# One score product, 16-tile value products, two-bank projections and a new PSUM bank plan in a recurrent attention kernel

## The chip, the cores and the metric

The kernel runs on one core of one Trainium2 chip. The metric is the device time of one execution in microseconds (us).

Engine names: PE is TensorE's matmul row, PEld its weight-load row, DVE is VectorE, ACT is ScalarE, SP is the queue that issues most of the DMAs. PSUM is the memory into which every matmul of these kernels writes (`ps` in the profile), used in banks by the program; SBUF is where the program keeps its other tiles. "L518" is line 518 of the kernel at hand; the lines of the two kernels differ, and the text says which stage a line is.

## The reference

A transformer block: layernorm, a recurrent attention with a small memory, a residual, layernorm, a gated feed-forward, a residual. Only the recurrence matters here:

```python
# S=2048 tokens, D=640, H=32 heads of Dh=128, M=8 memory tokens, segments of 32 tokens; all bf16
mem = mem0                                            # [1, 8, 640]
for s in range(64):
    h = concatenate([mem, x[:, 32*s : 32*s+32]])      # 40 tokens
    q, k, v = h@Wq, h@Wk, h@Wv                        # 32 heads x 128
    scores = q @ k.T * Dh**-0.5                       # 40 x 40 per head; mask: see below
    p = softmax(where(mask, scores, -1e9))            # memory rows see all, token rows memory + causal
    o = (p @ v) @ Wo                                  # 40 x 640
    mem = o[:, :8]                                    # goes into the next segment
    outs.append(o[:, 8:])
# ... then the feed-forward: h2 = h + (relu(n@W_gate) * (n@W_up)) @ W_down,  F = 1728
```

The loop is serial: segment s+1 needs `mem`, which is what the output projection of segment s made.

## The kernel before

One pass of the loop handles one segment. A pass projects the 8 memory tokens of its own segment together with 24 "rider" tokens of later segments, 32 in all; rings hold the riders' keys, queries and values (`Kr`, `Qr`, `Vr`). The tokens that don't fit (32 of every 128) are projected by "fillers", placed where TensorE would wait. In a pass, all but the transposes is cut into 32-column tiles of TensorE's array (`128*32`, `32*32` and `8*32` in the profile before; the transposes have `128*128`). A `Px` or `Pm` is an exponent of scores, `oT` the transposed attention output, `act_r` the transposed input of a pass.

Projection of one half (2048 of 4096 columns) into one PSUM bank, 20 matmuls of 512 columns, each with its own weight load:

```python
def qkv_bank(act, akeys, j, i, dst, dkey, eng):
    b = BQ[nq[0] % 2]                                  # two banks in turn
    nq[0] += 1
    def f(pe):
        for c in range(DC):                            # DC = 5
            for g in range(4):
                o = 2048 * i + 512 * g
                ins = pe.matmul(bank(b)[32 * g:32 * g + 32, :], act[:, c, :], W[:, j, c, o:o + 512],
                                start=(c == 0), stop=(c == DC - 1), skip_group_check=True)   # L330
    # ... then a copy of the bank to SBUF, on ACT and DVE in turn
```

Scores: two sweeps over the same keys, one with the 8 memory queries (`QmT`), one with the 32 rider queries (`Qr`); 64 load-matmul pairs each:

```python
def scores_mem(s):      # for k in 8, g in 4:
    pe.matmul(bank(BM)[..., k * 8:k * 8 + 8],      KmT[:, 4 * k + g, :],      QmT[:, 4 * k + g, :], ...)      # L469
    pe.matmul(bank(BM)[..., 64 + k * 8: ... + 8],  Kr[:, 4 * k + g, p:p + 32], QmT[:, 4 * k + g, :], ...)     # L472
    # Pm = exp(bank), then Pbd = min(Pm, block-diagonal mask)
def scores_x(s):        # for k in 8, g in 4:
    pe.matmul(bank(XS)[..., k * 32:k * 32 + 32],   Kr[:, 4 * k + g, p:p + 32], Qr[:, 4 * k + g, p:p + 32], ...)   # L536
    pe.matmul(bank(XS)[..., 256 + k * 32: ...],    KmT[:, 4 * k + g, :],       Qr[:, 4 * k + g, p:p + 32], ...)   # L539
    # Px = exp(bank), then causal min
```

Rider value products, 64 pairs on the four diagonal 32x32 tiles of the array, into three banks, then a reciprocal and a multiply per bank (L568, L579, L581):

```python
for k in ks:
    for a in range(2):                                 # a: memory keys or segment keys
        for g in range(4):
            pe.matmul(bank(XPB[k])[32 * g:32 * g + 32, o:o + 129], lh, rh, start=(a == 0), stop=(a == 1),
                      skip_group_check=True, tile_position=(32 * g, 32 * g))
```

The chain that closes the recurrence: output projection (L518, 128 pairs), copy of its bank to SBUF (L380), DVE transpose (L455), copy into `act_r` (L457). And the order of one pass:

```python
K, K, Q, Q, V            # projections, then trans8 of K and Q, then the second V half
scores_mem; filler 0 / half of woe; pv_mem; scores_x; filler 1 / half of woe
trans_om; trans_ox(s-1); wo_pass; to_act(s+1); pv_x(s); closing transpose of the filler
```

`woe` is the output projection of the leftover tokens, once in four passes (s mod 4 = 1); the layernorm of the next 128 rows is in the same pass.

The softmax here doesn't subtract the row's maximum and nothing guards it: scores larger than these inputs give would overflow.

## Time and profile before

The median is 1435.8 us (four executions, 1433.1 to 1438.6). The view by windows splits the profiled execution at the first projection of the first full pass and at the end of the last one. Columns: window, its length, then busy us (and instructions) of PE, PEld, DVE, ACT, POOL, then the granted clock, the DMA share and GB/s.

```profile
0.00:66.70 66.70, 33.72 (x756) 20.20 (x756) 17.07 (x51) 11.91 (x20) 4.11 (x21) 0.95 0.87 325
66.70:1187.50 1120.80, 1001.00 (x33927) 664.79 (x33923) 521.62 (x1449) 345.56 (x606) 0.00 (x0) 0.99 0.09 20
1187.50:1438.60 251.10, 219.79 (x1836) 118.21 (x1832) 92.28 (x189) 53.80 (x110) 0.00 (x0) 0.94 0.17 55
```

So 78% of the time is the passes: 1120.8 us, in which PE is busy 1001 us and DVE and ACT half of that or less. The chain that ended last, by engine, says the same:

```profile
PE 78%; DVE 7%; issue 6%; DMA 4%; ACT 3%; SPq 1%; POOL 0%; DVEq 0%; POOLq 0%
```

| before | us | from |
|---|---|---|
| start / passes / feed-forward | 66.7 / 1120.8 / 251.1 | windows |
| one pass, K projection to next K projection, mean of 62 | 18.08 | timeline |
| the same for s mod 4 = 1, 2, 3, 0 | 19.52, 18.23, 17.49, 16.96 | timeline |
| one projection matmul of 512 columns, start to start | 0.054 | timeline |
| one score sweep of 64 pairs | 0.53 | timeline |
| rider value product, 64 pairs, when undisturbed | 1.05 | timeline |

The groups of instructions, by shape, show the two score sweeps. The columns are line, engine, operation, tiles, shapes and count; then busy us and mean ns of one; then the idle time before them and what ended it.

```profile
L539 PE MATMUL ps<-Qr,KmT 128*32 128x32 bf16 x2048 | 45.3, 180 | 4.7 <-issue 4.6
...
L536 PE MATMUL ps<-Qr,Kr 128*32 128x32 bf16 x2048 | 44.6, 181 | 12.7 <-issue 12.7
...
L472 PE MATMUL ps<-QmT,Kr 128*32 128x8 bf16 x2016 | 40.7, 171 | 0.0
L469 PE MATMUL ps<-QmT,KmT 128*32 128x8 bf16 x2016 | 40.6, 171 | 2.0 <-issue 1.4
```

An 8-column matmul is listed with 171 ns and a 32-column one with 181 ns, yet 64 pairs take 0.53 us, 8.3 ns a pair. So the listed length is some 20 times what a pair adds, and four times the columns cost 10 ns of it.

Waits of PE, with total us, times and the longest:

```profile
PE ps L568 <- issue: 27.7, 30, 1.6
...
PE ps L518 <- DVE oT_102 L380: 22.6, 27, 2.7
...
PE ps L518 <- issue: 19.9, 20, 2.0
...
PE ps L536 <- issue: 12.7, 11, 1.6
...
PE ps L518 <- DVE oT_101 L380: 10.2, 31, 0.7
```

"Issue" means that nothing in the profile was waited for. These waits are odd: they fall into the middle of a matmul sequence. This is one, in a rider value product (timeline; start, duration, engine and group, and in brackets the idle time before it):

```profile
665.01 0.22 PE L568 MATMUL ps<-Vr_93,Px 32*32 32x129 bf16 x2
665.07 0.33 DVE L380 CAST wtok_108<-ps 128x160 bf16<-128x160 f32 x1 [2.19 <-PE ps L518]
665.43 0.35 DVE L455 STREAM_TRANSPOSE TBf<-wtok_108 128x160 bf16<-128x160 bf16 x1
665.81 0.17 DVE L457 COPY act_r_80<-TBf 128x40 bf16<-128x40 bf16 x1
666.12 0.09 PEld L568 LDWEIGHTS ps<-Vr_93,Px 32*32 32x32 bf16 x2 [1.07 <-issue]
```

The product stops after two matmuls for 1.07 us with everything it reads long there. Of the 80 "issue" gaps over 0.3 us in which both rows of TensorE stand, 79 are at the same place of its instruction order, number 193 modulo 256, counting loads, matmuls and the 107 semaphore instructions of its queue (without these the number drifts). And the page's list of DMA queues has an instruction queue that moved 285 packets of 16 KB (kind, packets, MB, share of the DMA engines):

```profile
q8 instruction: 285, 4.67, 1.3%
```

### The profile page before, as it was taken

How to read it: one execution, taken by the hardware profiler on the slowest of the kernel's cores; microseconds unless marked ns; L12 is line 12 of the kernel's file. 1: busy time of each engine (PE TensorE's matmuls, PEld its weight loads, DVE VectorE, ACT ScalarE, POOL GpSimd, SP SyncE). 2: the span in 40 equal slices, each digit the busy share in tenths (PEclk: the TensorE clock that was granted, in tenths of full speed). 3: DMA queues.
4: the chain of work that ended last, by engine and by line, in shares of the span. 5: the costliest groups of instructions: out<-in, count | busy, mean ns of one | idle time of the engine just before them, and what ended most of it. 6: DMA issues, size and time to landing. Idle time of an engine off the chain costs nothing.

```text
span 1438.6 us, 77225 instructions
## 1 busy us (share of the span) xinstructions
PE 1254.5 (87%) x36507; PEld 803.2 (56%) x36507; DVE 631.0 (44%) x1687; ACT 411.3 (29%) x736; POOL 4.1 (0%) x21
## 2 busy tenths in 40 slices
PE   1989898989898989898989898989898984899998
PEld 0555555655666556555656555556565653455454
DVE  2344444444444444444544454444454534334422
ACT  0223232323232323333333333333333321213311
POOL 1000000000000000000000000000000000000000
PEclk9999999999999999999999999999999997899999
DMA  9600000000000000000000000000000015110100
GB/s 368 236 16 22 18 21 18 21 18 22 18 22 18 22 18 22 17 21 18 22 18 22 19 21 18 21 18 22 18 20 18 17 39 202 40 37 24 51 19 19
DMA packets 44733, 58.21 MB, mean 40 GB/s; under 512 B 19264, under 2 KB 33280, under 8 KB 44416
## 3 DMA queue, kind: packets, MB, share of 16 engines
q1 hardware_dynamic: 40384, 42.80, 10.4%
q10 hardware_dynamic: 4032, 10.49, 2.0%
q8 instruction: 285, 4.67, 1.3%
q14 instruction: 32, 0.26, 0.1%
HBM read 35.48 MB, written 5.24 MB: 28 GB/s over the span
## 4 chain that ended last, share of the span: by engine, by line
PE 78%; DVE 7%; issue 6%; DMA 4%; ACT 3%; SPq 1%; POOL 0%; DVEq 0%; POOLq 0%
PE ps L330 23%; PE ps L518 13%; PE ps L350 11%; PE ps L804 8%; PE ps L364 6%; PE ps L568 5%; PE ps L826 5%; DMA W<-in_A_Wv_dram 3%; DVE tok_87 L337 1%; PE ps L539 1%; PE ps L493 1%; PE ps L536 1%; SPq L298 1%; PE ps L472 1%; ACT Kr L378 1%
## 5 line engine op out<-in xcount | busy, mean ns | idle before, releaser
L330 PE MATMUL ps<-W,act_r_81 128*32 128x512 bf16 x2680 | 156.1, 386 | 11.5 <-DMA W<-in_A_Wk_dram 8.5
L330 PE MATMUL ps<-W,act_r_80 128*32 128x512 bf16 x2560 | 149.6, 386 | 1.7 <-issue 1.6
L335 ACT ACTIVATE tok_84<-ps 128x512 bf16<-128x512 f32 x65 | 38.8, 597 | 362.1 <-PE ps L330 362.1
L330 PEld LDWEIGHTS ps<-W,act_r_81 128*32 128x32 bf16 x2680 | 69.8, 98 | 84.4 <-DMA W<-in_A_Wk_dram 8.8
L518 PE MATMUL ps<-Wo,oT_102 128*32 128x160 bf16 x4224 | 85.2, 238 | 27.8 <-DVE oT_102 L380 22.6
L330 PEld LDWEIGHTS ps<-W,act_r_80 128*32 128x32 bf16 x2560 | 67.7, 98 | 71.5 <-issue 8.9
L337 DVE CAST tok_87<-ps 128x512 bf16<-128x512 f32 x92 | 63.7, 692 | 98.4 <-PE ps L330 95.6
L581 DVE TENSOR_TENSOR ox<-ps,rx 128x384 bf16<-128x384 f32 (+1 forms) x192 | 98.5, 513 | 6.6
L518 PEld LDWEIGHTS ps<-Wo,oT_102 128*32 128x32 bf16 x4224 | 76.3, 99 | 35.8 <-DVE oT_102 L380 27.6
L518 PE MATMUL ps<-Wo,oT_101 128*32 128x160 bf16 x4224 | 83.9, 236 | 13.4 <-DVE oT_101 L380 10.2
L335 ACT ACTIVATE tok_86<-ps 128x512 bf16<-128x512 f32 x92 | 54.9, 597 | 116.6 <-PE ps L330 116.6
L350 PE MATMUL ps<-W,act_r_81 128*32 128x512 bf16 x1360 | 85.9, 380 | 1.9 <-issue 1.5
L518 PEld LDWEIGHTS ps<-Wo,oT_101 128*32 128x32 bf16 x4224 | 74.6, 98 | 22.0 <-DVE oT_101 L380 15.7
L350 PE MATMUL ps<-W,act_r_80 128*32 128x512 bf16 x1280 | 80.9, 380 | 0.0
L337 DVE CAST tok_85<-ps 128x512 bf16<-128x512 f32 x65 | 45.0, 692 | 69.7 <-PE ps L330 69.7
L378 ACT ACTIVATE Kr<-ps 128x768 bf16<-128x768 bf16 (+3 forms) x74 | 52.4, 724 | 38.5 <-DVE KmT L380 37.0
L544 ACT ACTIVATE Px<-ps 128x512 bf16<-128x512 f32 x64 | 38.2, 597 | 70.0 <-PE ps L539 70.0
L536 PE MATMUL ps<-Qr,Kr 128*32 128x32 bf16 x2048 | 44.6, 181 | 12.7 <-issue 12.7
L350 PEld LDWEIGHTS ps<-W,act_r_81 128*32 128x32 bf16 x1360 | 34.4, 96 | 34.8 <-issue 2.0
L518 PE MATMUL ps<-Wo,oTe 128*32 128x160 bf16 x2048 | 43.2, 233 | 11.8 <-issue 11.8
L378 ACT ACTIVATE Qr<-ps 128x768 bf16<-128x768 bf16 (+3 forms) x74 | 52.1, 723 | 1.5 <-PE ps L364 1.5
L539 PE MATMUL ps<-Qr,KmT 128*32 128x32 bf16 x2048 | 45.3, 180 | 4.7 <-issue 4.6
(193 smaller groups left out, 2077.3 us busy)
## 6 DMA issues: line engine op xcount, KB each, us to landing
attn_d<-wtoke SPq DMA_DIRECT2D x256, 2.5 KB
W<-in_A_Wk_dram ACTq DMA_DIRECT2D x1, 2560.0 KB
W<-in_A_Wq_dram ACTq DMA_DIRECT2D x1, 2560.0 KB
W<-in_A_Wv_dram ACTq DMA_DIRECT2D x1, 2560.0 KB
Wo<-in_A_Wo_dram ACTq DMA_DIRECT2D x1, 2560.0 KB
W<-in_A_Wk_dram SPq DMA_DIRECT2D x1, 2560.0 KB
W<-in_A_Wq_dram SPq DMA_DIRECT2D x1, 2560.0 KB
W<-in_A_Wv_dram SPq DMA_DIRECT2D x1, 2560.0 KB
```

Of the source, the lines that this page charges most:

```text
L330: ins = pe.matmul(bank(b)[32 * g:32 * g + 32, :], act[:, c, :], W[:, j, c, o:o + 512], start=(c == 0), stop=(c == DC - 1), skip_group_chec ...
L335: add("act", lambda a: a.activation(dst, bank(b), ACTF.Copy), r=[B(b)], w=[dkey])
L337: add("dve", lambda v: v.tensor_copy(dst, bank(b)), r=[B(b)], w=[dkey])
L350: ins = pe.matmul(bank(b)[32 * g:32 * g + 32, :], act[:, c, :], W[:, 2, c, o:o + 512], start=(c == 0), stop=(c == DC - 1), skip_group_chec ...
L364: ins = pe.matmul(bank_bf(b)[:, k * 128:(k + 1) * 128], t[:, (k % 4) * 128:(k % 4 + 1) * 128], ident[:, :], is_transpose=True)
L378: add("act", lambda a: a.activation(dst, src, ACTF.Copy), r=r, w=w)
L518: i = pe.matmul(bank(bk)[32 * gg:32 * gg + 32, 0:160], src[:, hb, :], w[:, gg], start=(hb == 0), stop=(hb == 31), skip_group_check=True)
L539: i = pe.matmul(bank(XS)[32 * g:32 * g + 32, 256 + k * 32:256 + k * 32 + 32], KmT[:, 4 * k + g, :], Qr[:, 4 * k + g, p:p + 32], start=True ...
L568: i = pe.matmul(bank(XPB[k])[32 * g:32 * g + 32, o:o + 129], lh, rh, start=(a == 0), stop=(a == 1), skip_group_check=True, tile_position=( ...
L581: add("dve", lambda v, src=src, k0=k0, n=n: v.tensor_tensor(ox[:, k0:k0 + n, :], src[:, :, 0:128], ap(rx, k0, [[1, n], [0, 128]]), ALU.mul ...
L804: ins = pe.matmul(bank(bk)[0:nf, :], w[:, c, j * 128:j * 128 + nf], xn2T[par][:, c, :], start=(c == 0), stop=(c == DC - 1))
L826: i = pe.matmul(bank(bk)[:, 0:320], hT[par][0:nf, j, u * 128:(u + 1) * 128], Wd[0:nf, j, hf * 320:(hf + 1) * 320], start=(j == 0), stop=(j ...
```

## The change

The intent is fewer and denser TensorE instructions and shorter waits:

1. One score product. The ring of queries keeps the 8 memory queries beside the 32 riders (`Qr` is [H, 3, 40]), so each key tile is loaded once and meets 40 columns: 64 pairs instead of 128.
2. Rider value products on all 16 tiles of 32x32, each row group into its own bank, with one reciprocal and two multiplies instead of three and three.
3. A projection does both halves, in two banks, with the same `act` tile; the second half's matmuls carry `ldweights=False` and use the tile that is loaded (`HOLD`). 40 loads fewer per pass.
4. The closing chain transposes straight from PSUM in fp32; the copy to SBUF rows goes to ACT, off the chain.
5. Filler evictions all on ACT; exponent of the memory scores ahead of the ring copy of the queries; the transposes of the layernormed rows behind `trans_ox`; `woe` as a filler unit. A new plan of the banks (`P0` to `P3`) makes room for all this.

```diff
+    def project(act, akeys, j, halves, banks):
         def f(pe):
             for c in range(DC):
-                for g in range(4):
-                    o = 2048 * i + 512 * g
-                    ins = pe.matmul(bank(b)[32 * g:32 * g + 32, :], act[:, c, :], W[:, j, c, o:o + 512], ...)
+                for n, i in enumerate(halves):
+                    for g in range(4):
+                        o = 2048 * i + 512 * g
+                        a = (bank(banks[n])[32 * g:32 * g + 32, :], act[:, c, :], W[:, j, c, o:o + 512])
+                        if n == 0 or not HOLD:
+                            ins = pe.matmul(*a, start=(c == 0), stop=(c == DC - 1), skip_group_check=True)
+                        else:
+                            ins = again(pe, *a, c == 0, c == DC - 1, g)      # ldweights=False
 ...
-    # scores_mem and scores_x
+    def scores(s):
+        # for k in 8, a in 2, g in 4:
+                        if a == 0:
+                            o, lh = bank(P0)[32 * g:32 * g + 32, 40 * k:40 * k + 40], Kr[:, h, 32 * q:32 * q + 32]
+                        else:
+                            o, lh = bank(P1)[32 * g:32 * g + M, 40 * k:40 * k + 40], KmT[:, h, :]
+                        i = pe.matmul(o, lh, Qr[:, h, q, :], start=True, stop=True, skip_group_check=True)
 ...
-                            i = pe.matmul(bank(XPB[k])[32 * g:32 * g + 32, o:o + 129], lh, rh, ...,
-                                          tile_position=(32 * g, 32 * g))
+            # for kh in 2, a in 2, c in 4 (k = 4 * kh + c), g in 4:
+                            i = pe.matmul(bank(P0 + g)[32 * c:32 * c + 32, 129 * kh:129 * kh + 129], ...,
+                                          tile_position=(32 * g, 32 * c))
 ...
-        wo_pass(oT[par], [("oT", par, "m"), ("oT", par, "x")], BM, wtok[par], ("wtok", par), "dve")
+        wo_pass(oT[par], [("oT", par, "m"), ("oT", par, "x")], T1)
         if not last:
-            to_act(s + 1, ("wtok", par), wtok[par])
+            to_act(s + 1, B(T1), bank(T1)[:, 0:160])
         if s >= 2:
+            wo_rows(T1, wtok[par], ("wtok", par), "act")
             store_attn(wtok[par], ("wtok", par), M, 32 * (s - 2), RID)
 # ... cut: bank plan, start of the program, layernorm split in two, filler units, layout of ox
```

## The prediction

> **What bounds the kernel now.** The windows view splits the 1438.6 us span into 66.7 us of start, 1120.8 us of recurrent passes (62 periods of 18.08 us, counted from one K projection to the next) and 251.1 us of feed-forward. In the passes TensorE's matmul row is busy 1001 us, VectorE 522, ScalarE 346, DMA 9%. The chain of waits puts 78% on PE, 7% on DVE, 6% on "issue". So a pass is TensorE's instruction stream plus gaps.

> From the timeline, an ordinary pass is: projections K, Q, V 120 matmuls at 54 ns = 6.5 us; filler projection 2.2; transposes 1.9; memory scores 0.53; rider scores 0.53; value products 0.24 (memory) and 1.05 (riders); output projection 2.33; together 15.2 us. The rest is gaps. Summed over the passes, TensorE idled 119 us: 72 us "issue", 32 us before the output projection waiting for DVE's oT, 6 us for Pbd. Every long "issue" gap (40 over 0.3 us, mean about 1 us) stands at the same place modulo 256 in TensorE's instruction order, and the instruction DMA queue moved 285 packets of 16 KB (73,014 loads and matmuls / 256 = 285). Where stalled, successive boundaries lie about 3.1 to 3.8 us apart. So dense stretches are bound by instruction supply.

> **What changes, per pass.**
> 1. One score product: 128 load-matmul pairs become 64 of 40 columns. At 8.3 ns per pair, -0.53 us.
> 2. Rider value products on 16 tiles: 64 pairs at 16.4 ns become issue-bound at about 8.3 ns, -0.5 us. [...]
> 3. Held tiles: 40 of about 1,110 instructions fewer; projections already run at 54 ns, a quarter of a 512-column stream, so their time stays. With 1, about 165 instructions fewer per pass (62,270 in all against 73,014). Fewer 256-blocks (3.5 against 4.3 a pass): issue stalls 72 -> about 55 us.
> 4. Chain after the output projection: PSUM copy (0.33) + transpose (0.35) + copy (0.17) loses the copy: 1.15 -> about 0.8 us. It must shrink, because the value product covering it shrinks to 0.55 us; passes without a closing transpose should wait about 0.25 us for act_r.
> 5. Filler evictions go to ScalarE, so oT is no longer behind a 0.69 us cast: the 0.33 us wait of ordinary passes mostly goes. The layernorm pass (s mod 4 = 1) keeps its about 1.7 us wait. In s mod 4 = 2, the row transposes move into a wait and the Q ring copy after the exponent.

> DVE normalising: 3+3 operations (2.05 us) become 1+2 (about 1.55), off the chain.

> **Sum.** -1.03 (1, 2) -0.25 (stalls) -0.3 (oT, Pbd) +0.1 (act_r) = about -1.5 us per pass; x62 = -93. In the start, projection and transposes of one row set alternate without filler: six evictions exposed at about 0.7 us, +4 us. Feed-forward unchanged. Predicted 1435.8 - 93 + 4, rounded to **1345 us**, range 1315 to 1375; chances: faster 0.94, within 2% 0.05, slower 0.01.

> **What would show it.** Period about 16.5 us; score group about 0.53 us per pass, once; rider value products about 0.55 us; projection spacing still 54 ns although loads fall to 29,795; "issue" gaps still at one residue modulo 256, about 55 us; waits of the output projection for oT under 1 us except in every fourth pass; projections waiting for act_r briefly; start about 71 us.

> **What would make it wrong.** 16 tiles not overlapping (value product stays 1 us: +30 us); instruction supply eating the gain, since output projection and value product together are now denser (+20 to +40); a slow fp32 transpose from PSUM lengthening the chain; held tiles slowing or quickening the projections.

The sum is: -1.03 - 0.25 - 0.3 + 0.1 = -1.48 us a pass, times 62 about -92 (booked as -93), and 1435.8 - 93 + 4 = 1346.8, rounded to 1345. The -0.5 us of point 2 is the estimate, that on 16 tiles the value product would come down from the 16.4 ns a pair of the trace before (1.05 us / 64) to the 8.3 ns of its score sweeps (0.53 us / 64); nothing before the change showed that it would. "Issue-bound" there has no more behind it than that pace. "A quarter of a 512-column stream": in the feed-forward of the trace before, 512-column matmuls on `128*128` start 216 ns apart (L804), and 54 ns is a quarter of it. "Instruction supply", here and in the expectations below, is the author's reading of the stops at one place in 256 and of the 285 packets; no run changed these packets themselves, so what holds TensorE there is not shown.

## The result, and the profile after

The median after is 1314.7 us (four executions, 1313.2 to 1317.6). Ratios in this document are the mean time of one kernel's fast runs over that of the kernel before in the same rounds, so not quite the ratio of the medians quoted: here 0.9159, with a 95% interval of 0.9135 to 0.9182. That is 8.4% faster, 121 us, where 91 were predicted.

The windows, cut at the same events:

```profile
0.00:69.40 69.40, 31.64 (x692) 12.22 (x512) 18.47 (x54) 12.06 (x20) 4.11 (x21) 1.00 0.84 312
69.40:1062.70 993.30, 924.43 (x29955) 552.71 (x27475) 439.77 (x1185) 418.23 (x763) 0.00 (x0) 1.00 0.10 22
1062.70:1312.90 250.20, 218.00 (x1839) 116.23 (x1812) 91.49 (x182) 54.06 (x111) 0.00 (x0) 0.94 0.17 56
```

All of the gain is in the passes, 1120.8 to 993.3 us. The start is 2.7 us longer, the feed-forward the same. In the passes PE's busy time fell by 77 us and its idle time by 51 us. The chain by engine: DVE's share went from 7% to 3%, "issue" from 6% to 4%.

```profile
PE 86%; issue 4%; DVE 3%; DMA 3%; ACT 1%; SPq 1%; POOL 0%; DVEq 0%; POOLq 0%; ACTq 0%
```

The instruction queue and the score groups (62,270 loads and matmuls are 243.2 blocks):

```profile
q8 instruction: 244, 4.00, 1.2%
```

```profile
L475 PE MATMUL ps<-Qr,Kr 128*32 128x40 bf16 x2048 | 42.5, 185 | 0.0
L475 PE MATMUL ps<-Qr,KmT 128*8 128x40 bf16 x2048 | 42.3, 179 | 0.0
```

The four score groups of before are two, of 40 columns; together they are 64 pairs a pass, which take 0.52 us. Waits of PE:

```profile
PE ps L557 <- issue: 28.6, 30, 2.0
...
PE ps L533 <- DVE oT_101 L374: 18.7, 15, 1.8
```

```profile
PE ps L533 <- issue: 9.9, 12, 1.3
```

L557 is the rider value product, L533 the output projection. The output projection's wait for `oT` is gone from all passes but the one with the layernorm (15 waits, one in four passes, mean 1.2 us). The "issue" waits inside the scores are gone; those inside the value product are as before (27.7 and 28.6 us). An undisturbed value product with the closing chain beside it:

```profile
624.46 0.28 PE L557 MATMUL ps<-Vr_91,Px 32*32 32x129 bf16 x16
...
624.52 0.28 PE L557 MATMUL ps<-Vp_95,Px 8*32 8x129 bf16 x16
624.58 0.35 DVE L455 STREAM_TRANSPOSE TBf<-ps 128x160 f32<-128x160 f32 x1 [1.15 <-PE ps L533]
...
624.71 0.35 PE L557 MATMUL ps<-Vr_91,Px 32*32 32x129 bf16 x16
...
624.84 0.35 PE L557 MATMUL ps<-Vp_95,Px 8*32 8x129 bf16 x16
...
624.96 0.18 DVE L456 CAST act_r_81<-TBf 128x40 bf16<-128x40 f32 x1
...
625.12 0.40 PE L358 MATMUL ps<-ident,tok_86 128*128 128x128 bf16 x4
```

From 624.45 (its first load) to 625.12 it takes 0.67 us where it took 1.05. The DVE transpose reads fp32 from PSUM in 350 ns (345 ns for bf16 from SBUF), and `act_r` is written at 625.14, 0.56 us after the transpose began.

**A better measure of the seams.** For each of the seams (instruction 193 modulo 256) in the passes, take the start of the instruction there minus the start of the one before it, and subtract the 90th percentile of the same spacing of that line's instructions elsewhere. This counts the whole stop, also what the listed ends hide. The result, in us over the passes:

| stop at a seam, in | before | after |
|---|---|---|
| rider value product | 34.1 | 33.8 |
| output projection (with woe) | 27.2 | 13.6 |
| scores | 20.9 | 0 |
| projections | 12.6 | 8.3 |
| other | 11.0 | 3.9 |
| sum (per pass) | 105.8 (1.71) | 59.6 (0.96) |
| seams per pass; of them stopping | 4.29; 115 of 266 | 3.63; 66 of 225 |

The idle column, which I had used for the prediction, gives 77 us before (the prediction had read 72) and 48 after. After, all 51 "issue" gaps over 0.3 us are again at number 193 modulo 256. And the stages of a pass, TensorE's starts to starts, mean of 62 passes:

| stage, us per pass | before | after | difference |
|---|---|---|---|
| projections | 6.67 | 6.59 | -0.08 |
| scores | 1.62 | 0.75 | -0.87 |
| fillers and woe | 2.65 | 2.32 | -0.33 |
| memory value product | 0.25 | 0.36 | +0.11 |
| transposes, with the waits behind them | 2.66 | 2.41 | -0.25 |
| output projection | 2.59 | 2.38 | -0.21 |
| rider value product | 1.64 | 1.21 | -0.43 |
| sum | 18.08 | 16.02 | -2.06 |

2.06 us times 62 is 128 us, of which the longer start gave some back. Put the two tables together: the scores' -0.87 is one sweep (0.53) and the stops in the scores (20.9 / 62 = 0.34). The value product's -0.43 is all its own, since its stops are unchanged. The output projection's -0.21 is its stops (13.6 / 62 = 0.22). In all, stops account for -0.75 of the -2.06.

### The profile page after: what moved, and what is told of

Same layout as the page of the kernel before. It is cut to its first block, busy times and chain, and to the rows that moved or that the text cites. A ratio compares the mean times of both kernels' runs of the same rounds, so it can differ in the third digit from the quotient of the medians.

```text
span 1312.9 us, 66508 instructions
## 1 busy us (share of the span) xinstructions
PE 1174.1 (89%) x32475; PEld 681.2 (52%) x29795; DVE 549.7 (42%) x1420; ACT 484.4 (37%) x894; POOL 4.1 (0%) x21
## 4 chain that ended last, share of the span: by engine, by line
PE 86%; issue 4%; DVE 3%; DMA 3%; ACT 1%; SPq 1%; POOL 0%; DVEq 0%; POOLq 0%; ACTq 0%
PE ps L339 30%; PE ps L533 14%; PE ps L325 11%; PE ps L831 9%; PE ps L358 6%; PE ps L853 5%; PE ps L557 3%; PE ps L475 2%; PE ps L366 2%; DMA W<-in_A_Wk_dram 2%; PE ps L508 1%; SPq L300 1%; PE ps L316 1%; DVE st L304 1%; PE ps L520 1%
## 5 line engine op out<-in xcount | busy, mean ns | idle before, releaser
L339 PE MATMUL ps<-W,act_r_81 128*32 128x512 bf16 x2660 | 222.1, 385 | 11.2 <-DMA W<-in_A_Wk_dram 8.5
L339 PE MATMUL ps<-W,act_r_80 128*32 128x512 bf16 x2540 | 208.7, 380 | 2.9 <-issue 2.8
L339 PEld LDWEIGHTS ps<-W,act_r_81 128*32 128x32 bf16 x2660 | 73.7, 97 | 149.8 <-issue 95.6
L325 PE MATMUL ps<-W,act_r_81 128*32 128x512 bf16 x1380 | 140.8, 389 | 0.9 <-issue 0.9
L339 PEld LDWEIGHTS ps<-W,act_r_80 128*32 128x32 bf16 x2540 | 70.1, 96 | 128.6 <-issue 85.2
L325 PE MATMUL ps<-W,act_r_80 128*32 128x512 bf16 x1300 | 129.6, 379 | 0.3 <-issue 0.3
L533 PE MATMUL ps<-Wo,oT_101 128*32 128x160 bf16 x4224 | 81.1, 235 | 19.8 <-DVE oT_101 L374 18.7
L372 ACT ACTIVATE tok_86<-ps 128x512 bf16<-128x512 f32 x94 | 56.2, 598 | 104.6 <-PE ps L325 103.6
L533 PEld LDWEIGHTS ps<-Wo,oT_101 128*32 128x32 bf16 x4224 | 73.8, 98 | 25.5 <-DVE oT_101 L374 21.3
L374 DVE CAST tok_85<-ps 128x512 bf16<-128x512 f32 x67 | 46.4, 692 | 96.9 <-PE ps L325 96.9
L374 DVE CAST tok_87<-ps 128x512 bf16<-128x512 f32 x64 | 44.3, 692 | 94.8 <-PE ps L325 94.8
L568 DVE TENSOR_TENSOR ox<-ps,rx 128x512 bf16<-128x512 f32 x128 | 82.5, 686 | 2.2
L372 ACT ACTIVATE Kr<-ps 128x768 bf16<-128x768 bf16 (+3 forms) x89 | 68.0, 775 | 34.9 <-DVE KmT L374 17.8
L533 PE MATMUL ps<-Wo,oT_100 128*32 128x160 bf16 x4224 | 79.7, 233 | 0.8 <-issue 0.4
L372 ACT ACTIVATE Qr<-ps 128x512 bf16<-128x512 bf16 (+3 forms) x110 | 68.9, 659 | 17.9 <-PE ps L358 16.7
L533 PEld LDWEIGHTS ps<-Wo,oT_100 128*32 128x32 bf16 x4224 | 72.6, 97 | 5.1 <-issue 1.0
L339 PE MATMUL ps<-W,act_e_82 128*32 128x512 bf16 x960 | 61.0, 380 | 0.0
L455 DVE STREAM_TRANSPOSE TBf<-ps 128x160 f32<-128x160 f32 x64 | 22.4, 350 | 88.3 <-PE ps L533 88.3
L339 PE MATMUL ps<-W,act_e_83 128*32 128x512 bf16 x840 | 53.4, 380 | 0.0
L533 PE MATMUL ps<-Wo,oTe 128*32 128x160 bf16 x2048 | 43.8, 233 | 8.6 <-issue 8.6
L374 DVE COPY KmT<-ps 128x256 bf16<-128x256 bf16 x64 | 18.7, 292 | 60.7 <-PE ps L358 60.7
```

The lines of the kernel that those rows point to most:

```text
L325: return pe.add_instruction(mybir.InstMatmult(name=nc.get_next_instruction_name(), engine=mybir.EngineType.PE, ins=[pe.lower_ap(rhs), pe.l ...
L339: ins = pe.matmul(*a, start=(c == 0), stop=(c == DC - 1), skip_group_check=True)
L372: add("act", lambda a: a.activation(dst, src, ACTF.Copy), r=r, w=w)
L374: add("dve", lambda v: v.tensor_copy(dst, src), r=r, w=w)
L533: i = pe.matmul(bank(bk)[32 * gg:32 * gg + 32, 0:160], src[:, hb, :], w[:, gg], start=(hb == 0), stop=(hb == 31), skip_group_check=True)
L568: add("dve", lambda v, kh=kh: v.tensor_tensor(ox[:, :, kh, :], src[:, :, kh, 0:128], ap(rx, kh, [[2, 4], [0, 128]]), ALU.mult), r=[B(P0 + ...
```

## The experiments

The theory after the result: about a third of the gain came from TensorE standing less at seams of its instruction stream, and this hangs on how many instructions are packed into the dense stretches and where the seams fall. The rival: the seams are a bystander, and the parts of the change add up by the work they take away. Twelve kernels were run, all correct, each timed in four executions beside seven of the kernel before. "At the scale of 1435.8" below means a ratio times 1435.8; half widths of the intervals are about 3 to 8 us. The runs were on five chips, on which the kernel before had medians from 1437 to 1450 us; stops and stages are read from one trace of each kernel and are not scaled.

| run | what | ratio (95%) | against after, us | seam stops, us |
|---|---|---|---|---|
| after | the change | 0.9159 (0.9135 to 0.9182) | 0 | 59.6 |
| a_hold_off | loads not held | 0.9214 (0.9177 to 0.9250) | +8 | 58.6 |
| b_four_tiles | value product on 4 tiles | 0.9264 (0.9232 to 0.9296) | +15 | 49.2 |
| c_two_products | scores in two sweeps | 0.9838 (0.9790 to 0.9885) | +97 | 122.2 |
| d_copy_first | copy before the transpose | 0.9199 (0.9161 to 0.9237) | +6 | 56.1 |
| e_filler_dve | second filler eviction on DVE | 0.9263 (0.9225 to 0.9301) | +15 | 56.8 |
| f_aligned | seams moved, all passes | 0.9170 (0.9125 to 0.9215) | +2 | 44.3 |
| g_misaligned | as f, seams half a block off | 0.9492 (0.9454 to 0.9530) | +48 | 104.4 |
| h_start | start pipelined | 0.9155 (0.9111 to 0.9200) | -1 | 63.7 |
| i_ln_late | layernorm issued later | 0.9161 (0.9120 to 0.9201) | 0 | 85.2 |
| j_aligned_light | seams moved, 3 passes of 4 | 0.9029 (0.8974 to 0.9084) | -19 | 43.8 |
| k_late_and_aligned | i and j | 0.9031 (0.8975 to 0.9087) | -18 | 64.6 |
| n_before_one_product | before, with part 1 alone | 0.9361 (0.9319 to 0.9403) | +29 | 56.2 |

### Undoing one part

**Held tiles.** `HOLD = False`: every matmul loads its tile again, 2,680 loads more, ten blocks more.

```diff
-    HOLD = True
+    HOLD = False
```

> The changed kernel with its held tiles undone: every projection matmul loads its own weights again (40 more load instructions in each pass, nothing else). My theory (time is the matmul stream at its measured spacing plus waits plus instruction-supply stalls at every 256th TensorE instruction): projection matmuls stay at 54 ns each, the 40 loads hide, only the supply stalls grow a little, by about 8 us in all; total about 1322 us. Rival (dropping the loads is what quickens the projections, half of the pass): spacing of the projection matmuls rises and the total goes up by 30 us or more, to 1345 or above.

Measured 1323.7 us, 8 us more than after, give or take about 6. The seam stops did not rise (58.6 us) and the projections were 0.07 us a pass longer in the trace. The held tiles are worth little: projections run at 54 ns a matmul with or without them, and these 2,680 added instructions, among matmuls 54 ns apart, cost 3 ns each, give or take 2 (8 us / 2,680).

**Four tiles.** The value product back on the diagonal, with the copies of its transposed output reordered to match (not shown), all else as after.

```diff
-                            i = pe.matmul(bank(P0 + g)[32 * c:32 * c + 32, 129 * kh:129 * kh + 129],
+                            i = pe.matmul(bank(P0 + k // 2)[32 * g:32 * g + 32, 129 * (k % 2):129 * (k % 2) + 129],
 ...
-                                          skip_group_check=True, tile_position=(32 * g, 32 * c))
+                                          skip_group_check=True, tile_position=(32 * g, 32 * g))
```

> The changed kernel with the rider value products put back on the four diagonal array tiles, same number of instructions, same banks and VectorE operations. My theory: the product goes from about 0.67 us to about 1.05 us without stalls, +0.4 us in each of 64 passes, and since it covers part of the chain copy-transpose it loses a little less: total 1336 to 1342 us. Rival (product is bound by issue or by instruction supply, not by tiles): no change over 8 us.

Measured 1332.2 us, +15 us, less than expected. The value product became 0.34 us a pass longer (1.21 to 1.55), but the seam stops fell by 10 us (59.6 to 49.2). So the 16 tiles save about 25 us of the product's own time (0.34 us a pass, and 4.5 us of its own stops that were fewer here), and 10 of these come back as stops.

**Two score products.** The same layout, banks and order as after, but two sweeps, with 8 and with 32 columns:

```diff
-            for k in range(8):
-                for a in range(2):
+            for lo, hi in ((0, M), (M, M + SEG)):
+                for k in range(8):
+                    for a in range(2):
 ...
-                        i = pe.matmul(o, lh, Qr[:, h, q, :], ...)
+                            i = pe.matmul(o, lh, Qr[:, h, q, lo:hi], ...)
```

> The changed kernel with one score product split again into two sweeps (8 columns, then 32 columns) into the same banks, at the same place: 64 more load-matmul pairs, 128 more instructions in each pass. My theory: +0.51 us of issue in each pass (+32 us) and more supply stalls, because 256 score instructions now run in about 1 us, below the 3 to 3.5 us that a block of 256 needs: stalls +15 to +25 us; total 1360 to 1372 us. Rival (small matmuls are free behind other work): under +15 us.

Measured 1417.2 us, +97 us, about twice of what was expected. The second sweep itself is 0.53 us a pass, 33 us. The stops rose from 59.6 to 122.2 us, 63 us. Together they are 96 of the 97; between the two traces themselves, spans of 1312.9 and 1418.7 us, the difference is 106 us, so some 10 us stay unexplained there. The waits view of this run has them where the instructions are dense, not only in the scores (L558 the value product, L534 the output projection, L476 the scores):

```profile
PE ps L558 <- issue: 40.9, 36, 2.1
...
PE ps L534 <- issue: 27.7, 27, 1.9
...
PE ps L476 <- issue: 8.7, 15, 2.0
```

A sweep is 128 instructions, half a block. Successive seams are rarely under 2.8 us apart (5th percentile of the spacing, before 2.75, after 2.81). The packets of the instruction queue show a floor directly: in the traces before and after no two of the 16 KB packets start less than 3.2 us apart (shortest 3.24 before, 3.28 after). So half a block is worth about 1.6 us where the packets set the pace (an estimate: half of the 3.24 to 3.28 us; that they do is not shown directly), against 0.53 us of matmuls; the 97 us are 1.56 us a pass. This is where the rival falls: the same 40 columns for each key tile, cut in twice as many instructions, cost three times the matmul time that was added.

**The score product alone, put into the kernel before.** The opposite test, so that the answer does not hang on the other parts (the rider scores so move ahead of the memory value product, as in after):

```diff
-            scores_mem(s)
+        scores(s)               # 64 pairs of 40 columns into banks XP1, XS
+            exp_mem()
 ...
-        scores_x(s)
+        exp_x()
```

> The kernel before with the one score product alone: same banks for everything else, same value products, same chain, same fillers; 64 load-matmul pairs (128 instructions) fewer in each pass. Counting matmul time alone, 64 pairs at 8 ns: -0.5 us a pass, -32 us, 1404 us. Supply theory (undoing this part in the changed kernel cost 102 us, of which 63 us were stalls at the 256-instruction boundaries): stalls fall too, by 30 to 60 us, total 1345 to 1375 us.

Measured 1355.9 us beside 1449.8 of the kernel before on that chip, ratio 0.9361: 92 us at the scale of 1435.8. The stops fell from 105.8 to 56.2 us and the pass from 18.08 to 16.75 us. Between the traces, spans of 1438.6 and 1355.7 us, it is 83 us: the sweep's 33 and the 50 of the stops. So this one part of the change has two thirds (traces) to three quarters (ratios) of its gain, and all of the fall of the stops; everything else together takes the stops no further (59.6 us after).

**Copy before the transpose.** The chain as before: copy to SBUF rows on DVE, then the transpose.

```diff
+        wo_rows(T1, wtok[par], ("wtok", par), "dve")
         if not last:
-            to_act(s + 1, B(T1), bank(T1)[:, 0:160])
+            to_act(s + 1, ("wtok", par), wtok[par][:].rearrange("p c t -> p (c t)"))
-            wo_rows(T1, wtok[par], ("wtok", par), "act")
# ... cut: TBf in bf16, and the same order at the start of the program
```

> The changed kernel with the chain behind the output projection as it was before: VectorE copies the PSUM rows to bf16 first, then transposes, then copies (+0.35 us on the chain). My theory: exposed only in the passes without a closing transpose (s mod 4 of 0 and 1, where the trace shows the next projection starting 53 ns after the copy), about +0.3 us in half of the passes where no supply stall covers it: +6 to +10 us, total 1321 to 1325 us. Rival (the shortened chain is the main gain): +0.35 us in every pass, 1336 us.

Measured 1323.9 us, +6 us, with 5.8 us of it in a wait that the kernel after does not show, projections for `act_r`:

```profile
PE ps L339 <- DVE act_r L456: 5.8, 17, 0.4
```

The size came as expected, but as a time it is at the edge of the noise (0.0040 of ratio, give or take about 0.0045 from the two intervals); the wait is clear in the trace. It says why the chain had to get shorter: the shorter value product no longer covers the old one. There are 17 waits in 62 passes; in most passes a closing transpose or a stop at a seam still covers it.

**Second filler eviction on DVE.**

```diff
-                return lambda: to_v(BQ[i], Vr[q], i, ("Vr", q), "act")
+                return lambda: to_v(BQ[i], Vr[q], i, ("Vr", q), ("act", "dve")[i])
 ...
-            return lambda: to_tok(BQ[i], 2 + i, "act")
+            return lambda: to_tok(BQ[i], 2 + i, ("act", "dve")[i])
```

> The changed kernel with the second eviction of each filler projection put back on VectorE, ahead of the copy of the memory outputs. My theory: the output projection waits some 0.3 us more for oT in the three of four passes that have a filler: +10 to +16 us, 1325 to 1331 us. Rival (that wait was never exposed): under +4 us.

Measured 1329.3 us, +15 us: the 0.69 us cast stands in front of `oT` on DVE again, and the output projection and the transposes before it wait (46 waits for `oT` instead of 15; transposes 0.21 us a pass longer):

```profile
PE ps L533 <- DVE oT L374: 28.9, 46, 1.8
```

The five undone parts add up to 8 + 15 + 97 + 6 + 15 = 141 us, more than the 121 us of the whole. So the parts do not simply add up, though the five intervals together would nearly allow it; the sum is weak evidence, the stops in b and c are the better one.

### Moving the seams

If a stop hangs on where a seam falls, the same work with shifted seams must change time. In these kernels some projection matmuls of 512 columns are cut into two to four narrower ones, which adds instructions and no columns, at a place where TensorE's matmuls are far apart (54 ns, against about 8 ns a pair in the scores).

```diff
-    def project(act, akeys, j, halves, banks):
+    def project(act, akeys, j, halves, banks, extra=0):
+        # cuts: which matmuls of c > 0 are made of 2, 3 or 4 narrower ones, until `extra` instructions are added
 ...
-                        a = (bank(banks[n])[32 * g:32 * g + 32, :], act[:, c, :], W[:, j, c, o:o + 512])
+                        for lo, hi in zip(b, b[1:]):
+                            a = (bank(banks[n])[32 * g:32 * g + 32, lo:hi], act[:, c, :], W[:, j, c, o + lo:o + hi])
```

**Aligned and misaligned.** Both make each pass a whole number of blocks, 38 blocks more in all than after; f puts a seam 71 instructions ahead of the output projection, g half a block later. The number of instructions differs by 128 in the whole program.

```diff
+    EXTRA = [0, 168, 134, 128, 128, 226, 134, 128, 128, 226, ...]     # f_aligned
+    EXTRA = [0,  40, 134, 128, 128, 226, 134, 128, 128, 226, ...]     # g_misaligned
```

> The changed kernel with 128 to 226 more TensorE instructions in each pass and no more work: projection matmuls of Q and of V's first half are cut into up to four narrower ones, so that each pass holds a multiple of 256 instructions and the 256-instruction boundaries always fall 71 instructions before the output projection. Supply theory: every block then lasts about 3.5 us or more by itself, the gaps at the boundaries nearly vanish (48 us to under 12 us) and the kernel gets FASTER with more instructions: 1272 to 1290 us. Rival (instruction count as such, or loads and matmuls, costs time): some 140 more instructions in each pass at 4 to 8 ns make it slower, 1345 us or more.

> The same extra cuts in each pass as in the aligned kernel, except that the first of them is 128 instructions shorter, so that all later boundaries fall half a block off: one inside the output projection (57 instructions in), the next 199 instructions before the following one. Supply theory: a stall of 1.0 to 1.5 us in nearly every pass, 60 to 90 us of gaps; 1340 to 1370 us, 60 us or more above the aligned kernel. Rival (position does not matter): within 6 us of the aligned kernel.

Measured 1318.4 us for f and 1363.3 us for g: 45 us between two programs that differ only in where the seams fall. In g nearly every pass stops inside the value product, 83 us of stops in it; the timeline of one (L573 the value product):

```profile
635.16 0.28 PE L573 MATMUL ps<-Vr,Px 32*32 32x129 bf16 x16
...
635.23 0.26 PE L573 MATMUL ps<-Vp,Px 8*32 8x129 bf16 x12
...
635.67 0.18 DVE L472 CAST act_r<-TBf 128x40 bf16<-128x40 f32 x1
...
636.34 0.24 PE L573 MATMUL ps<-Vp,Px 8*32 8x129 bf16 x4 [0.86 <-issue]
636.35 0.10 PEld L573 LDWEIGHTS ps<-Vp,Px 8*32 8x32 bf16 x3 [1.00 <-issue]
...
636.36 0.28 PE L573 MATMUL ps<-Vr,Px 32*32 32x129 bf16 x16
```

Twelve matmuls of the second group, a stop until 636.34, then the other four; `act_r` was written in the meantime. In f the value product takes 0.71 us a pass instead of 1.21, and the ordinary passes are faster (15.51, 15.25, 14.55 us for s mod 4 = 2, 3, 0, against 16.10, 15.49, 14.91 after). But I had expected 1272 to 1290 us, and f gained nothing: the fourth pass went from 17.47 to 18.66 us. Its woe puts another 256 instructions into it, and f added 226 more: its woe took 3.72 us against 2.86, its output projection 3.17 against 2.46. So the prediction of f failed mainly in the pass that already held the most instructions; j below, which adds none there, bears this out. A part of it is the clock: the four executions of f average 0.977 (those of after 0.985, of g 0.984), and its fastest, at 0.983, took 1310.3 us. That is about 8 us (an estimate), still far from 1272 to 1290.

**Aligned in the three ordinary passes.** So j adds instructions only in the ordinary passes, 106 to 128 each (more in the first and in one at the end), and lets the fourth pass alone; the seams come 55 to 85 instructions ahead of the output projection. 22 blocks more than after.

```diff
+    EXTRA = [0, 182, 106, 128, 126, 0, 106, 128, 126, 0, ...]
```

> The changed kernel with cuts of Q and V matmuls (106 to 128 more instructions, no more work) in the three ordinary passes of four and none in the densest fourth pass, so that the last 256-instruction boundary before each output projection lies 55 to 85 instructions ahead of it in every pass. In the trace of the changed kernel the passes that happen to have that distance take 16.7, 15.3, 14.84 and 14.4 us (s mod 4 of 1, 2, 3, 0), against means of 17.5, 16.1, 15.5 and 14.9. Supply theory: the period falls from 16.02 to about 15.4 us, total 1272 to 1288 us, and boundary stalls fall from 60 to about 25 us. Rival (the earlier aligned kernel gained nothing because position is not what costs): 1310 us or more.

Measured 1305.5 us beside 1444.7, ratio 0.9029: 1296 us at the scale of 1435.8, 19 us less than after, and the intervals of the two ratios, each against the kernel before on its own chip, do not overlap. This version beats both kernels, with about 5,800 more instructions than after. The traces show less of it: the pass went from 16.02 to 15.80 us, 14 us over 62 passes. I had expected 15.4 us a pass and 1272 to 1288 in all, so it is half the gain or less. Stops fell to 43.8 us, now mostly in output projection and woe (33.7 of them): output projection and value product are one and a half blocks (256 and 128 instructions) in about 2.8 us, so no placement keeps a seam out of them.

### Other waits

**The layernorm behind the value product.** The one wait left by name, 18.7 us for `oT` in the fourth pass, comes from the layernorm's work on DVE ahead of it. In i that front is issued after the value product.

```diff
-        if s % 4 == 1 and ln:
-            ln1_front(nb, xt, ("xt",))
         if last:
 ...
         pv_x(s)
+        if s % 4 == 1 and ln:
+            ln1_front(nb, xt, ("xt",))
```

> The changed kernel with the layernorm of the next rows (every fourth pass) issued behind the rider value product instead of ahead of the copy of the memory outputs, nothing else. My theory: the wait of the output projection for oT, 1.2 us in each of 16 passes in the trace, goes; some of it returns as supply stalls since these passes are the densest: -8 to -17 us, 1298 to 1307 us. Rival (that wait is covered by a supply stall anyway): within 4 us of the changed kernel.

Measured ratio 0.9161, no gain at all, where 8 to 17 us were expected. The wait did go (the transposes of the fourth pass took 0.60 us instead of 1.83). The stops rose from 59.6 to 85.2 us, in the output projection and the value product that follow:

```profile
PE ps L557 <- issue: 38.8, 30, 2.0
...
PE ps L533 <- issue: 22.7, 26, 1.8
```

Against 28.6 and 9.9 us after, 23 us more. So the 1.23 us that the transposes lost, about 20 us over 16 passes, came back as 26 us of stops, and the wait cost nothing here. Why the one takes the place of the other is not shown.

**Both.** k is the edit of i with cuts like those of j, but others in number (101, 142 and 117 instructions instead of 106, 128 and 126), which put the seams 57 to 90 instructions ahead.

> Both: the layernorm issued late, and cuts that hold the last 256-instruction boundary 57 to 90 instructions ahead of the output projection. Each was tried alone: the late layernorm gained nothing, since supply stalls took back the wait that it removed; the placement alone gave a ratio of 0.903. Supply theory: with the boundaries placed, part of the removed wait (TO and output projection in every fourth pass, about 1.4 us) is kept, since about 0.6 to 0.9 us of it is not needed by the supply: -10 to -16 us against the placement alone, ratio 0.892 to 0.898. Rival (the fourth pass is bound by supply alone): ratio 0.900 to 0.905.

Measured ratio 0.9031, the same as j. The fourth pass went from 17.30 to 16.80 us but the others lost about 0.2 us each, and stops were 64.6 us. The layernorm wait is worth nothing also here, though the cuts differ, so what the others lost is not separated from them.

**The start.** h computes projections one row set ahead of the transposes, to cover the evictions that the new start exposes. (The edit also makes the transpose of the closing chain name the bank that it reads; this is not shown.)

```diff
+    todo = [("p", 0), ("p", 1), ("t", 0), ("p", 2), ("t", 1), ("t", 2)]
-        for n, (a, ks) in enumerate(ex_act + [(a0, k0)]):
+        for what, n in todo:
```

> The changed kernel with the start pipelined: projections of one row set are issued before the transposes of the row set before it. My theory: of six exposed evictions about 0.7 us each, four are covered, the start ends 2 to 4 us earlier; 1311 to 1313 us, within the scatter. Rival (the start is bound by the weight DMAs): no earlier.

In the trace the start is back at 66.6 us from 69.4. The time did not change (ratio 0.9155), but an interval of 6 us either way cannot show 3 us: inconclusive as a time, clear in the trace.

## Why the prediction was right or wrong

The call, faster by over 2%, was right. The time, 1345 us, was 30 us too high, and the result lies 0.3 us under the low end of the range (the mean of its four executions, 1315.0, lies on it).

- One score product, -0.53 us of matmul time: right. One sweep of 64 pairs takes 0.52 us with 40 columns as with 8 or 32.
- Value products "issue-bound at about 8.3 ns", 0.55 us: nearly. Undisturbed they take 0.66 us (10 ns a pair), so -0.4 instead of -0.5 us. From 4 tiles to 16, with 129 columns and a load per matmul, this case shows 1.05 to 0.66 us, a factor of 1.6.
- Projections still at 54 ns: right, before and after. Held tiles give no time there.
- Waits for `oT` and `Pbd`, -0.3 us: right in kind (the only `oT` wait left is the fourth pass, 18.7 us; e shows the part of the evictions, 15 us).
- "passes without a closing transpose should wait about 0.25 us for act_r", +0.1 us: did not come. The chain from the last start of the output projection to the written `act_r` went from 1.20 to 0.85 us and the product covers it but for some 0.05 us. d shows the wait that the old chain would have made.
- Start +4 us: +2.7. Feed-forward unchanged: right (251.1 and 250.2 us).
- All long "issue" gaps at one residue modulo 256: right.

**The step that failed** is the sum's supply term: "Fewer 256-blocks (3.5 against 4.3 a pass): issue stalls 72 -> about 55 us", booked as -0.25 us a pass. That the stops would stay at one place in 256 and would fall was right, the size was not. Measured between starts the stops went from 105.8 to 59.6 us, -0.75 us a pass; the missing 0.5 us a pass is 31 us, the whole error. Two mistakes are in it. First, 72 us was read from the idle column (77 in fact), in which the listed ends of matmuls hide part of each stop (a projection matmul is listed with 380 ns and the next one starts 54 ns after it). Second, I scaled it with the number of blocks. In the idle column itself the fall was from 77 to 48 us, 0.47 us a pass; so of the missing 0.5 about 0.2 belongs to the scaling and 0.3 to what that column hides. The experiments show that density and place count: one sweep of scores less took 50 us of stops away in n and one more added 63 in c; 38 blocks more, in the projections, left the time of f as it was; and half a block's shift in g cost 45 us.

What is shown, and what isn't: that the stops stand at one place in 256 (79 of the 80 long gaps before, all 51 after), that there is one 16 KB packet per 256 instructions (285 for 73,014, 244 for 62,270), and that they follow density and placement, is measured. That TensorE stands because its next block has not come is inference, and is not shown. What the trace has beside it: a packet of the instruction queue takes about 1.0 us (0.88 to 1.4 for 19 in 20), and the instruction at a stopped seam starts 1.26 to 1.56 us after the end of the latest packet, whereas at seams without a stop it is 1.3 to 4.8 us (5th to 95th percentiles, before). No experiment changed these packets themselves. Nor was a run without recording compared; all times here are of recorded executions, and whether the stops are as long without recording is open.

## What to carry to other kernels

Where TensorE works on many tiny matmuls (here pairs 8 to 10 ns apart), count its instructions per stretch as well as its columns: here half a block (128 instructions) in a dense stretch cost 92 to 97 us over 62 passes by the ratios (83 to 106 between traces), about three times its matmul time, and a merged product with more columns was the largest gain. Measure stops between starts at every 256th instruction, not in idle columns, before removing any wait in front of a dense stretch: in i the wait removed came back as 26 us of stops. Here, moving the seams by cutting matmuls in the projections gained another 19 us (14 in the traces), at the price of a placement that any later edit upsets.
